# A new order of steps behind the first loads, in a kernel of chunked attention and a phase-mixing layer

## The chip, the cores and the metric

The program runs on one core of a Trainium2 chip. The core has TensorE (matrix products; "PE" in the profile, and "PEld" for its loads of weights), VectorE ("DVE"), ScalarE ("ACT"), GpSimd ("POOL") and SyncE ("SP", which only issues transfers). The engines run side by side, each through its own list of instructions in order, and wait for each other on semaphores. Transfers between the chip's main memory and the core's own memory run on 16 DMA engines. They are issued from POOL (the loads, which also turn 32-bit values into 16-bit ones, and some stores), from SP (stores, and DMA transposes, which turn a tile of 16-bit values around on its way from one place of the core's memory to another) and from ACT (stores). The metric is the time of one execution in microseconds (us); less is better.

## What is computed

Attention inside chunks of 64 positions, for 8 batches, 8 heads, 576 positions and 64 values per head, and then a layer that mixes positions and channels:

```python
scores = scale * np.matmul(q_c, k_c.transpose(0, 1, 2, 4, 3))      # per chunk of 64
scores = scores - np.max(scores, axis=-1, keepdims=True)
attn = np.exp(scores)
attn = attn / (np.sum(attn, axis=-1, keepdims=True) + 1e-09)
out = np.matmul(attn, v_c)                    # then x = out as (batch, position, head*64)
theta = x @ w_theta
zr, zi = x * np.cos(theta), x * np.sin(theta)
y = np.einsum('ts,bsd->btd', w_tok_r, zr) + np.einsum('ts,bsd->btd', w_tok_i, zi)
u = x + y
return u + np.maximum(u @ w_ch, 0.0)
```

## The kernel before

The work goes by pairs of batches, p = 0 to 3. A pair's 2 x 576 positions make nine tiles of 128 rows. They are loaded and attended to in five groups: A (tiles 0 and 1) and B (tiles 2 and 3) of the first batch, C (tiles 4 and 5) and D (tiles 6 and 7) of the second, and M (tile 8), which holds the last 64 positions of both batches.

Everything that the core does is a list of steps, the text `ORDER` (lines 17 to 60). A step such as `V0.0D.4` names a kind of work (V0), a pair and a group (0D) or a pair and a tile, and the places that it uses (4: a bank of TensorE's result memory, of which there are eight, or a slot of the arrays `big`, `mid` or `uT`). The loop at line 711 goes through the list and calls the function of each step; each function gives its instructions to one engine, or to two. So the list is at once the order on every engine. Where a step reads what another wrote, or writes a slot or bank that another still reads, a wait is put in. Nothing else sets the order.

The kinds, in the order in which a group meets them:

- `qk` and `v` (lines 167 and 219) load queries and keys (two transfers of 256 KB; four of 64 KB for M) and values (one of 128 KB and two of 64 KB; two of 64 KB for M), all from POOL; `lw`, `lp`, `lc` load the weights. POOL takes the semaphores of its transfers in turn, eight of them, so that it can be at most eight transfers ahead of the landings.
- `T`, `Tq`, `Tk` (line 291, DVE) turn queries and keys in squares of 32; `S` (line 334, TensorE, 64 products of 32x64 for a group, 32 for M) makes the scores; `E` (line 350, ACT) the exponentials; `V0` and `V1` (line 376, TensorE, 16 products of 64x64 each, 8 for M) the products with the values of four heads; `N0` and `N1` (line 398, DVE) the divisions, which give x.
- `X` (line 415) turns x around on TensorE, and `xv` or `xa` copy the result out on DVE or ACT; or `xd` (line 432) does both in one DMA transpose from SP. `H` (line 453) multiplies by w_theta, `G` (line 474, ACT) takes cosine and sine, `Z` (line 491, DVE) makes zr and zi.
- `TW` (line 253) turns the weights over positions around, `twv` and `twa` copy them out. `Y` (line 540, nine products of 128x512; `Ya`, `Yb`, `Ym` are its parts) mixes the positions for one tile, and needs zr and zi of all its batch's groups and of M; `A` (line 548, DVE) adds x.
- `U` with `uv` or `ua`, or `ud` alone (line 562, a DMA transpose), turns the tile around once more; `W` (line 582, TensorE, four products of 128x512) multiplies by w_ch; `R` (line 586, DVE) makes the result; `st`, `sa` and `sg` (line 664) store it, issued from SP, ACT or POOL.
- `dm` are TensorE products that nobody reads.

A pair's groups are thus at different stages at any moment, and TensorE's list runs through blocks of different kinds and pairs. `crossed` (line 215) says which quarter of the array a chunk's scores go to: for all groups but 0A and 0B the second tile of a group has its two halves exchanged, and its values are loaded in two halves.

Of the kernel before, what the change touches and what calls it, by code (L numbers as in the profile page):

```python
# [17 lines left out]
on.00 init.00 qk1.0A.0 pre.00 qk0.0A.1 qk.0B.2 cy0.0A.3 cv1.0A qk.0M.4 T0.0A.1 S0.0A.0 Tq.0B.0  # L18
v.0A Tk.0B v.0M v.0B Tq.0M.5 lw.03.2 S.0B.2 T1.0A E0.0A.0 V0.0A.0 Tk.0M S1.0A.4 E1.0A S.0M.6
lp.00 E.0M.1 V0.0M.7 N0.0A V1.0M.6 qk.0C.4 N1.0M V1.0A.4 dm.2.0 E.0B.2 lw.01.5 V1.0B.2 V0.0B.0  # L20
N1.0A X.0A.4 qk.1M.1 lw.02.3 N1.0B N0.0B xa.0A.1 X.0B.5 TW.03.3 v.0C N0.0M X.0M.7 xv.0B.2
H1.0A.5 G1.0A.0 H1.0B.0 G1.0B.3 xv.0M.4 Tq.0C.2 Z1.0A H0.0A.7 qk.0D.0 lw.00.6 G0.0A.1 v.0D
twv.03 Z0.0A H.0M.5 H0.0B.4 G.0M.4 TW.01.6 G0.0B.1 Ya.03.3 Tk.0C S.0C.0 Z1.0B twv.01 v.1M E.0C.3
# [3 lines left out]
xv.0C.1 N1.0D V0.0D.4 H.0C.2 G.0C.1 qk.1D.3 V0.1M.6 N0.0D X.0D.4 xv.0D.3 v.1B N0.1M Z.0C Yb.00  # L27
v.1A Ym.00 v.1D H.0D.4 Ya.05.2 T.1B.4 G.0D.5 V1.1M.3 A.00 Ya.06.6 TW.04.0 S.1B.4 Ya.04.7 N1.1M
X.1M.3 E.1B.4 Z.0D Yb.06 T.1A.4 Ym.06 S.1A.4 qk.1C.6 A.06 Yb.05 T.1D.5 xv.1M.3 U.06.6 twv.04
E.1A.1 Ym.05 Ya.07.4 V1.1B.0 qk.2M.3 A.05 ua.06.3 N1.1B V0.1B.5 N0.1B Yb.04 lc.00 S.1D.2 v.1C  # L30
V1.1A.0 Yb.07 qk.2C.5 Ym.07 qk.2D.4 N1.1A E.1D.2 V0.1D.2 N0.1D X.1B.0 xa.1B.4 V1.1D.5 Ym.04
H.1M.1 H.1B.2 qk.2B.0 N1.1D V0.1A.5 A.07 qk.2A.2 qk.3B.1 Y.08.4 T.1C.7 A.04 N0.1A X.1A.5 U.04.6
G.1M.2 Z.1M xv.1A.1 U.00.7 S.1C.0 v.2M G.1B.6 E.1C.4 A.08 X.1D.5 xv.1D.2 v.2B W.06.2 R.06.3
U.07.0 H.1A.4 uv.04.3 V0.1C.2 v.3D uv.07.4 v.2A uv.00.5 W.00.7 G.1A.7 N0.1C U.05.0 U.08.6
uv.08.5 v.2C V1.1C.2 W.01.1 uv.05.6 H.1D.4 N1.1C X.1C.2 Z.1A Z.1B R.01.2 qk.3A.6 W.08.3 xa.1C.4
Y.10.0 H.1C.1 G.1D.7 Z.1D T.2M.8 T.2A.7 W.02.4 S.2M.5 v.3B G.1C.9 Z.1C R.02.4 E.2M.1 Y.13.6 A.13
T.2B.9 S.2A.1 W.04.4 R.00.0 Y.16.5 qk.3D.0 R.04.5 R.08.6 W.05.4 S.2B.6 T.2D.7 E.2B.7 T.2C.2
Y.11.3 A.11 R.05.8 A.16 W.03.6 R.03.9 Y.15.7 A.15 E.2A.10 V1.2A.5 A.10 S.2C.3 E.2C.11 V0.2M.1
N0.2M V1.2M.7 N1.2M Y.14.2 N1.2A V0.2B.3 N0.2B V0.2A.0 V0.2C.6 v.2D Y.17.5 A.14 A.17 V1.2C.2
# [4 lines left out]
W.16.0 st.08 qk.3C.8 T.3M.4 Y.25.1 T.3C.1 Y.24.5 Y.27.4 A.24 ud.13.1 G.2B.5 S.3B.5 A.25 W.14.1  # L44
R.14.3 Y.26.7 Z.2A S.3M.1 E.3B.6 E.3D.1 V1.3D.2 R.16.12 S.3C.5 A.27 Z.2B sa.07 ud.15.2 ud.12.6
ud.10.4 ud.18.5 W.18.0 E.3C.10 E.3M.7 Y.20.4 sa.17 A.26 V0.3M.7 R.18.11 V0.3C.0 N1.3D W.15.5
R.15.5 N0.3C st.14 S.3A.2 E.3A.3 W.12.6 Y.23.5 V1.3M.2 A.20 N0.3M N1.3M W.10.7 st.11 R.10.7
sa.10 R.12.13 V0.3D.3 N0.3D V1.3C.1 ud.25.3 N1.3C Y.28.0 W.13.4 st.16 ud.27.0 V1.3A.2 V0.3B.6
A.28 st.18 R.13.7 N1.3A Y.21.0 A.21 st.02 ud.24.2 Y.22.2 A.22 xd.3M.12 H.3M.0 V1.3B.3 sa.03
W.24.2 N0.3B N1.3B V0.3A.6 N0.3A ud.20.1 G.3M.10 W.25.1 xd.3D.9 H.3D.3 G.3D.7 xd.3C.1 Z.3M  # L50
H.3C.6 G.3C.5 Z.3D A.23 Z.3C ud.21.4 xd.3B.6 W.21.0 ud.22.3 sa.05 H.3B.3 G.3B.7 Z.3B ud.26.2
W.22.6 st.12 Y.34.7 R.25.8 W.26.3 R.24.6 sg.25 R.22.13 Y.35.1 A.35 R.26.1 R.21.8 xd.3A.10 W.27.6
W.20.2 H.3A.3 sg.21 st.01 st.00 Y.36.0 Y.37.1 R.20.0 sa.20 A.34 ud.28.4 W.28.7 ud.23.6 G.3A.7
A.36 Z.3A Y1.31.0 sa.13 Y.38.3 ud.34.3 A.37 ud.35.1 R.28.7 A1.31 st.24 A.38 W.34.0 Y0.31.7 A0.31
sg.22 ud.37.0 W.37.3 W.35.7 R.34.13 R.37.6 st.26 Y.32.0 A.32 U0.31.3 uv0.31.1 R.35.1 U1.31.1
Y.33.4 A.33 st.15 ud.36.4 W.36.7 W.23.3 R.27.5 ud.38.2 sg.35 sa.34 R.23.13 R.36.1 W.38.6 R.38.0
sa.37 sa.28 Y.30.4 Wp.31.6.7 uv1.31 sa.38 A.30 W0.31 ud.32.3 W.32.1 R0.31.7 sa0.31 R.32.6 U.30.6
sa.36 W1.31 uv.30.1 R1.31 st.27 ud.33.6 W.33.4 R.33.0 st.32 sa.33 W.30.6 sg.23 dm.2.7 R.30.13
st1.31 sa.30
# [4 lines left out]
def kernel(  # L64
# [137 lines left out]
    def cast_qk_half(f, engines):  # L202
        def cast(p, g, slot=None):
            if f == 0:
                st["qk", p, g] = big(slot).rearrange(
                    "p (f w h s d) -> p f w h s d", f=2, w=2, h=HH, s=2
                )
            t, to = st.pop(("stage", f)), st["qk", p, g][:, f]
            for w, e in enumerate(engines):
                copy = nc.scalar.copy if e == "a" else nc.vector.tensor_copy  # L210
                copy(out=to[:, w], in_=t[:, w])

        return cast

    def crossed(p, g):

        return int(p > 0 or g not in "AB")

    def load_v(p, g):
# [86 lines left out]
    def qk_t_half(f):  # L306
        def step(p, g, slot=None):
            if f == 0:
# [10 lines left out]
    def score_mms(ps, t, n, heads, cross):  # L319
        for h in range(heads):  # L320
            for e in range(2):
                for c in range(2 * n):
                    r, cc = (c // 2, c % 2) if n == 2 else (0, c)
                    to = cc ^ (r * cross)
                    nc.tensor.matmul(  # L325
                        ps[half[to], r, h],
                        t[quarter[c], 1, h, :, e],
                        t[quarter[c], 0, h, :, e],
                        start=(e == 0),
                        stop=(e == 1),  # L330
                        tile_position=(32 * c, CH * to),
                    )

    def scores(p, g, b):
# [413 lines left out]
```

## Time and profile before

| | |
|---|---|
| three executions | 195.51, 193.31, 194.77 us (median 194.77) |
| the profiled execution, first to last instruction (span) | 191.7 us |
| TensorE's granted clock | 1.000 throughout |
| instructions | 5957, 2579 of them products |
| HBM read and written | 33.06 MB and 9.44 MB |

The page gives the profiled execution's span alone; the executions' own times lie 1.6 to 3.8 us above it, which is what lies around the first and the last instruction and the spread between executions. In the profile's lines "L528" is line 528 of the kernel, "us" after a start is a duration, and what stands in brackets is the time for which the engine stood idle before, with what ended it. A product's record outlasts the time after which the next one may start, so blocks are best timed from start to start, or by the pieces of the chain of waits, which do not overlap.

### The profile page before, as it was taken

The page shows a single profiled execution, that of the slowest core. Times are in us where ns is not written, and L with a number is a line of the kernel's source. Part 1 is how long each engine was busy: PE and PEld are TensorE (multiplying, and loading weights), DVE is VectorE, ACT ScalarE, POOL GpSimd, SP SyncE. Part 2 cuts the span into 40 slices and gives each one's busy share as a digit, 9 for nine tenths or more (in the row PEclk, how much of TensorE's full clock was granted, in tenths as well). Part 3 has the DMA queues.
Part 4 walks back from the last instruction along what each step waited for, and adds up shares of the span by engine and source line. Part 5 has one row for each costly group of instructions (what it writes and reads, how often), then busy time and mean ns, then how long its engine had stood idle before and what let it go on. Part 6 is the DMA issues. An engine that isn't in the chain of part 4 may idle for free.

```text
span 191.7 us, 5957 instructions
## 1 busy us (share of the span) xinstructions
PE 173.9 (91%) x2579; PEld 91.1 (48%) x2579; DVE 138.8 (72%) x255; ACT 81.4 (42%) x100; POOL 88.4 (46%) x125
## 2 busy tenths in 40 slices
PE   0168899999999999999999969999999999999992
PEld 0155455645554655554555425454444444455450
DVE  0564789879779977996885968396686677553782
ACT  3113895476629946803218659142032560400000
POOL 8998289697798955799878000000000001100110
PEclk9999999999999999999999999999999999999999
DMA  5999999999999999999999986497356894885667
GB/s 159 202 157 182 188 132 143 164 177 165 151 153 183 175 182 181 157 116 152 164 133 132 196 145 168 82 197 222 74 158 126 112 281 103 246 230 150 180 173 259
DMA packets 103338, 31.86 MB, mean 166 GB/s; under 512 B 94672, under 2 KB 99152, under 8 KB 103312
## 3 DMA queue, kind: packets, MB, share of 16 engines
q0 software_dynamic: 76048, 17.33, 98.2%
q1 hardware_dynamic: 23872, 9.57, 23.9%
q10 hardware_dynamic: 3392, 4.59, 7.6%
q8 instruction: 20, 0.33, 0.7%
q14 instruction: 6, 0.05, 0.1%
HBM read 33.06 MB, written 9.44 MB: 222 GB/s over the span
## 4 chain that ended last, share of the span: by engine, by line
PE 78%; DMA 8%; DVE 4%; POOL 4%; issue 2%; ACT 1%; DVEq 0%; ACTq 0%; POOLq 0%
PE psum L528 35%; PE psum L573 14%; PE psum L449 12%; PE psum L325 6%; PE psum L389 5%; DMA out_dram<-mid 3%; PE psum L421 3%; DMA mid<-x 2%; DMA v<-in_v_dram 2%; PE psum L264 1%; POOL big L174 1%; PE psum L555 1%; POOL big L179 1%; DVE mid L578 1%; DVE x L406 1%
## 5 line engine op out<-in xcount | busy, mean ns | idle before, releaser
L528 PE MATMUL psum<-zr,wT 128*128 128x512 f16 (+2 forms) x185 | 62.6, 375 | 0.1
L528 PE MATMUL psum<-zi,wT 128*128 128x512 f16 (+2 forms) x184 | 59.6, 374 | 0.0
L528 PEld LDWEIGHTS <-wT 128*128 128x128 f16 (+1 forms) x369 | 31.3, 100 | 32.9 <-issue 0.5
L233 POOL DMA_DIRECT2D v<-in_v_dram x54 | 41.0, 787 | 10.1 <-DMA big<-in_k_dram 4.5
L672 POOL DMA_DIRECT2D out_dram<-mid x5 | 2.7, 551 | 75.3 <-DVE mid L578 75.3
L573 PE MATMUL psum<-wch,uT 128*128 128x512 f16 x140 | 35.1, 380 | 0.0
L550 DVE TENSOR_TENSOR x<-psum,x 128x512 f16<-128x512 f32 x35 | 23.7, 683 | 15.3 <-PE psum L528 15.1
L449 PE MATMUL psum<-wtheta,mid 128*128 128x512 f16 x144 | 33.2, 379 | 1.7 <-DMA mid<-x 1.7
L355 ACT ACTIVATE mid<-psum 128x1024 f16<-128x1024 f32 (+1 forms) x19 | 17.3, 930 | 33.9 <-PE psum L325 32.2
L578 DVE SCALAR_TENSOR_TENSOR mid<-psum,x 128x512 f32<-128x512 f32 (+1 forms) x37 | 23.9, 669 | 7.7 <-PE psum L573 5.6
L406 DVE TENSOR_TENSOR x<-psum,recip 128x512 f16<-128x512 f32 (+1 forms) x40 | 25.5, 638 | 1.4
L286 DVE STREAM_TRANSPOSE big<-big 128x1024 f32<-128x1024 f32 (+3 forms) x25 | 24.7, 1011 | 1.3 <-DMA big<-in_q_dram 0.9
L325 PE MATMUL psum<-big 32*64 32x64 f16 x1152 | 15.3, 199 | 9.5 <-DVE big L286 9.5
L471 ACT ACTIVATE big<-psum,pihalf 128x1024 f16<-128x1024 f32 x14 | 15.6, 1116 | 17.4 <-PE psum L449 17.4
L449 PEld LDWEIGHTS <-mid 128*128 128x128 f16 x144 | 13.9, 98 | 18.1 <-DMA mid<-x 2.2
L325 PEld LDWEIGHTS <-big 32*64 32x64 f16 x1152 | 13.0, 112 | 15.1 <-DVE big L286 10.1
L573 PEld LDWEIGHTS <-uT 128*128 128x128 f16 x140 | 12.4, 98 | 13.4 <-issue 0.8
L152 ACT ACT_TABLE_LOAD x12 | 15.4, 1283 | 6.3 <-DVE recip L404 4.8
L179 POOL DMA_DIRECT2D big<-in_q_dram x15 | 13.8, 920 | 1.7 <-DMA big<-in_k_dram 0.9
L472 ACT ACTIVATE big<-psum 128x1024 f16<-128x1024 f32 x14 | 14.3, 1024 | 0.0
L389 PEld LDWEIGHTS <-mid 64*64 64x64 f16 x576 | 8.9, 113 | 11.4 <-issue 9.0
L389 PE MATMUL psum<-v,mid 64*64 64x65 f16 x576 | 12.2, 202 | 2.0 <-DMA v<-in_v_dram 1.3
(51 smaller groups left out, 135.7 us busy)
## 6 DMA issues: line engine op xcount, KB each, us to landing
big<-in_q_dram POOLq DMA_DIRECT2D x15, 256.0 KB, 6.5
big<-in_k_dram POOLq DMA_DIRECT2D x15, 256.0 KB, 7.0
out_dram<-mid SPq DMA_DIRECT2D x13, 256.0 KB, 2.8
out_dram<-mid ACTq DMA_DIRECT2D x13, 256.0 KB, 3.0
v<-in_v_dram POOLq DMA_DIRECT2D x18, 128.0 KB, 5.7
v<-in_v_dram POOLq DMA_DIRECT2D x36, 64.0 KB, 6.1
out_dram<-mid POOLq DMA_DIRECT2D x5, 256.0 KB, 3.1
out_dram<-mid SPq DMA_DIRECT2D x5, 128.0 KB, 3.0
```

Of the source, the lines that this page charges most:

```text
L179: nc.gpsimd.dma_start(t[:, w].rearrange("p h s d -> p h (s d)"), ap[2 * p + bb, :, s0 : s0 + GT, :].rearrange("h (p s) d -> p h (s d)", s=2),)
L233: nc.gpsimd.dma_start(v16[rows, slot + t, :, 0:D], v[b, :, t0 : t0 + m, :].rearrange("h s d -> s h d"),)
L286: nc.vector.transpose(out.bitcast(FP32).rearrange("p (x l s) -> p x s l", l=32, s=2), in_.bitcast(FP32).rearrange("p (x s d) -> p x s d", ...
L325: nc.tensor.matmul(ps[half[to], r, h], t[quarter[c], 1, h, :, e], t[quarter[c], 0, h, :, e], start=(e == 0), stop=(e == 1), tile_position= ...
L355: nc.scalar.activation(out=eT[:, 0:n].rearrange("p r h i -> p (r h i)"), in_=st.pop(("ps_s", p, g)).rearrange("p r h i -> p (r h i)"), fun ...
L389: nc.tensor.matmul(ps[half[cc], r, h4, :], eT[rows, r, h, :], v16[rows, slot + r, h, 0 : D + 1],)
L406: nc.vector.tensor_tensor(out=x.rearrange("p r (h d) -> p r h d", h=HH), in0=ps[:, :, :, 0:D], in1=recip[:, 0:n].broadcast_to((P, n, HH, D ...
L449: nc.tensor.matmul(ps, xT[:, a, :], wtheta16[:, a, :], start=(a == 0), stop=(a == NDB - 1))
L528: nc.tensor.matmul(ps[half[b]] if j == MID else ps, w, z[:, cols], start=(kt == 0), stop=(kt == 2 * KT),)
L550: nc.vector.tensor_tensor(out=x, in0=st.pop(("ps_y", p, j)), in1=x, op=ALU.add)
L573: nc.tensor.matmul(ps, uT[:, a, :], wch16[:, a, :], start=(a == 0), stop=(a == NDB - 1))
L578: nc.vector.scalar_tensor_tensor(out=out, in0=ps, scalar=0.0, in1=x, op0=ALU.max, op1=ALU.add)
```

## The change

The list `ORDER` is replaced. The same 562 entries of the same kinds stand in it, with few differences: of the copies and stores some go to another engine (from DVE to ACT or back: the copies out after X for 0C, 1A, 1C, 1M, 2A, 2M, after TW for tile block 4 and after U for five tiles; and there are 17 whole stores from ACT instead of 15, 8 from POOL instead of 5, 10 from SP instead of 15). The steps up to `Ya.01`, at the end of the first pair's start, are the same and in the same order, except that `TW.02` now stands ahead of `Ya.01`, and with other slots. Behind that the order is new.

```diff
-on.00 init.00 qk1.0A.0 pre.00 qk0.0A.1 qk.0B.2 cy0.0A.3 cv1.0A qk.0M.4 T0.0A.1 S0.0A.0 Tq.0B.0
+on.00 init.00 qk1.0A.0 pre.00 qk0.0A.1 qk.0B.2 cy0.0A.5 cv1.0A qk.0M.15 T0.0A.3 S0.0A.0 Tq.0B.4 v.0A
...
-Z0.0B Ya.01.6 Yb.01 TW.02.4 twa.02 Z.0M Ym.01 T.1M.2 A.01 Yb.03 V0.0C.0 Ym.03 V1.0C.4 Tq.0D.1
-S.1M.6 E.1M.4 Ya.02.7 Yb.02 Ym.02 N1.0C Tk.0D S.0D.4 N0.0C A.03 TW.00.0 qk.1B.2 A.02 X.0C.3
-lw.04.0 E.0D.3 U.01.6 ua.01.0 U.02.4 ua.02.1 U.03.5 twv.00 Ya.00.0 V1.0D.6 uv.03.2 qk.1A.6
...
+H0.0B.6 G.0M.9 TW.01.2 G0.0B.10 Ya.03.7 Tk.0C S.0C.4 Z1.0B twv.01 v.1M E.0C.11 Z0.0B TW.02.0 Ya.01.6
+Z.0M Yb.03 V0.0C.2 V1.0C.4 twa.02 Yb.01 Ya.02.0 Ym.01 T.1M.16 Yb.02 S.1M.1 Tq.0D.17 E.1M.12 N0.0C
+Tk.0D S.0D.2 E.0D.13 Ym.03 N1.0C TW.00.4 X.0C.1 A.01 A.03 twv.00 Ym.02 A.02 V0.0D.6 N0.0D qk.1B.18
...
-N1.2C N0.2A N0.2C Y.18.4 xd.2C.12 S.2D.2 st.04 qk.3M.2 V1.2B.0 E.2D.1 X.2A.5 W.07.6 N1.2B v.3C
-V0.2D.0 R.07.7 N0.2D V1.2D.2 xa.2A.11 v.3A X.2M.7 X.2B.5 v.3M Y.12.6 A.12 N1.2D H.2A.0 xa.2M.10
-A.18 T.3A.7 H.2M.6 xa.2B.1 G.2M.13 T.3D.5 Z.2M H.2C.4 H.2B.6 G.2A.6 xd.2D.5 ud.16.4 G.2C.0 Z.2C
-ud.17.2 T.3B.9 H.2D.0 W.17.4 S.3D.2 G.2D.4 Z.2D ud.11.6 W.11.5 R.17.5 R.11.13 sa.06 ud.14.3
...
+V1.2B.2 N1.2B N0.2A N1.2C Y.18.0 S.2D.6 V0.2C.1 qk.3A.0 N0.2C X.2A.3 xd.2C.9 A.18 ud.11.9 X.2M.4
+xv.2M.13 E.2D.4 W.07.5 R.07.3 V1.2D.6 V0.2D.1 Y.12.0 T.3D.2 X.2B.4 xa.2B.1 H.2M.5 N1.2D S.3D.6 N0.2D
+H.2C.1 xv.2A.7 qk.3B.3 H.2A.3 ud.17.4 qk.3C.14 G.2M.4 xd.2D.13 W.17.5 G.2C.15 ud.18.2 qk.3M.7 A.12
+H.2D.0 Z.2C Z.2M G.2A.12 W.18.2 T.3C.8 H.2B.3 T.3B.18 ud.15.8 ud.16.1 G.2D.10 Z.2D Y.26.0 A.26 st.06
...
-sa.36 W1.31 uv.30.1 R1.31 st.27 ud.33.6 W.33.4 R.33.0 st.32 sa.33 W.30.6 sg.23 dm.2.7 R.30.13
-st1.31 sa.30
+st.23 W.32.5 R.32.3 sa.22 sa0.31 W.34.6 W.30.3 R.33.12 sa.37 sa.26 sg.32 R.34.13 sg.34 R.30.1 sg.30
+W.36.1 sa.35 R.36.10 sg.36 st.33 dm.2.7 st1.31 sa.27
```

On POOL the values of 3M are loaded much sooner, the pairs' values and queries are exchanged in places, and the last four loads are `qk.3A`, `qk.3B`, `qk.3C`, `qk.3M`. On SP the first transposes stand as `xd.2C`, `ud.11`, `ud.17`, `xd.2D`, `ud.18`, `ud.15`, `ud.16`, and only then comes the first store, `st.06`; before, `st.04` stood between `xd.2C` and `xd.2D`.

The functions change little. Which tile of a group has its halves exchanged now depends on the group (`turned`; the second tile for A and C, the first for B and D), and `load_v` follows it with the same number of transfers:

```diff
-    def crossed(p, g):
-
-        return int(p > 0 or g not in "AB")
+    def turned(p, g, r):
+
+        if p == 0 and g in "AB":
+            return 0
+        return r ^ int(g in "BD")
...
+            parts = []
+            for t in range(2):
+                t0 = s0 + t * P
+                if turned(p, g, t):
+                    parts += [(half[1 - i], t, 2 * p + bb, t0 + i * CH, CH) for i in range(2)]
+                else:
+                    parts.append((slice(0, P), t, 2 * p + bb, t0, P))
...
-        score_mms(ps, t, n, H, crossed(p, g))
...
+    def scores(p, g, b):
+        score_mms([score_parts(p, g, b)], size(g), H)
+
+    def scores_of_two(p, gs, *bs):
+
+        score_mms([score_parts(p, g, b) for g, b in zip(gs, bs)], 2, H)
```

`score_mms` has a loop over groups inside, so that a new kind of step, `SS`, could make the scores of two groups at once; no entry of the new list uses it. In five functions of halves the place is taken from whichever half comes first with a slot (`if slot is not None` for `if f == 0`), and the loop over the list reads names of two groups.

More of the change, by code (lines that the diff above doesn't have):

```diff
@@ L30 @@
[L30 to L35, printed above, removed]
@@ L48 @@
[L48 to L53, printed above, removed]
@@ L322, in score_mms, with score_parts @@
                 for c in range(2 * n):
[L323 to L334, printed above, removed]
+                    for p, g, ps, t in groups:
+                        r, cc = (c // 2, c % 2) if n == 2 else (0, c)
+                        to = cc ^ turned(p, g, r)
+                        nc.tensor.matmul(
+                            ps[half[to], r, h],
+                            t[quarter[c], 1, h, :, e],
+                            t[quarter[c], 0, h, :, e],
+                            start=(e == 0),
+                            stop=(e == 1),
+                            tile_position=(32 * c, CH * to),
+                        )
+    def score_parts(p, g, b):
         n = size(g)
@@ L387, in products @@
                     for cc in range(2):
-                        rows = half[cc ^ (r * crossed(p, g))]
+                        rows = half[cc ^ turned(p, g, r)]
                         nc.tensor.matmul(
@@ L653, in step @@
         def step(p, j, slot=None):
-            if f == 0:
+            if slot is not None:
                 st["o", p, j] = mid(slot, 1, FP32)
```

74 lines of the change are left out of this document (39 added, 35 removed).

## The prediction
> **What bounds the kernel now.** I read the page first (busy shares, the slices, the queues), then the chain of waits in order of time.
>
> ```profile
> span 191.7 us, 5957 instructions
> PE 173.9 (91%) x2579; PEld 91.1 (48%) x2579; DVE 138.8 (72%) x255; ACT 81.4 (42%) x100; POOL 88.4 (46%) x125
> ...
> PE   0168899999999999999999969999999999999992
> ...
> DMA  5999999999999999999999986497356894885667
> ...
> q0 software_dynamic: 76048, 17.33, 98.2%
> ...
> PE 78%; DMA 8%; DVE 4%; POOL 4%; issue 2%; ACT 1%; DVEq 0%; ACTq 0%; POOLq 0%
> ```
>
> TensorE is busy in every slice from the fifth to the last but one, and the chain lies on it for 78%. Beside it the DMA engines are full until slice 23, about 111 us, with POOL's loads (q0). So there are two clocks: TensorE's list, and the landings of the loads, which TensorE must not outrun. A gain can come from less time in TensorE's list, from its stalls, or from the ends. The chain shows all three:
>
> ```profile
> 27.60 0.68 DVE wT L274
> 28.28 0.05 issue
> 28.33 1.90 PE psum L528 x8
> ...
> 36.17 0.73 PE psum L264 x10
> 36.90 0.55 PE psum L421 x8
> ...
> 38.13 0.86 PE psum L528 x4
> ...
> 55.19 0.25 PE psum L389 x16
> ...
> 79.00 2.05 PE psum L528 x9
> 81.04 0.64 PE psum L325 x64
> 81.68 0.97 PE psum L573 x4
> 82.65 1.94 PE psum L528 x9
> 84.59 0.86 PE psum L573 x4
> ...
> 94.26 0.51 PE psum L389 x48
> ...
> 107.49 4.72 DMA mid<-x
> ...
> 112.26 1.90 PE psum L449 x8
> ```
>
> The reader is to see three things. A W block (L573) takes 0.86 after another large block, and 0.97 after an S block (L325); a Y block (L528) takes 1.94 or 2.05 in the same way; three V blocks in a row (L389 x48) take 0.51, where one by itself takes 0.25. So each boundary between S, V and the large blocks costs about 0.10. Without it S is 0.54, V 0.15, TW (L264) 0.62, X (L421) 0.45, a Y block's four products 0.87 and its last 0.22. And there is one long wait in mid-run, H.2D (L449) for the DMA transpose xd.2D.
>
> **The change, part by part.**
>
> *Boundaries.* The work on TensorE is the same. I count the places in the two lists where TensorE goes from one of the three kinds (S; V; all others) to another: 83 before, 59 after, because V blocks stand in threes and S blocks in twos and threes. 24 x 0.10 = -2.4 us, all of it on the path, since TensorE is the path. Ends: -0.6, if S next to S or V costs what it costs beside a large block, and -2.6.
>
> The Trainium skill, TensorEngine Tiling (Array Packing), section Key Properties, says that changing the tiling mode drains TensorE; its page TensorE: Matmul & The Clock Gate, section Single matmul latency, gives a constant of 398 cycles at 2.4 GHz, 0.17 us, for what a product takes beyond its columns. Taken as the price of a boundary that would be an estimated 24 x 0.17 = 4.1 us, and a sum 1.7 lower. The trace has 0.10 there, and it decides.
>
> *Stalls that go.* What released H.2D is seen in SP's own waits and in TensorE's row:
>
> ```profile
> SPq L433 <- DMA out_dram<-mid: 5.1, 1, 5.1
> ...
> 112.26 1.90 PE L449 MATMUL psum<-wtheta,mid 128*128 128x512 f16 x8 [1.67 <-DMA mid<-x]
> ```
>
> xd.2D writes mid slot 5, from which st.04 had to be stored first. In the new list no store is on SP before xd.2D, and xd.2D goes to slot 13. That frees TensorE's 1.67 and, since the next block's start is usually hidden, 1.8 from start to start. The wait for a weight copy at 28.28 (0.2) goes too, as TW.02 now stands in it. Together -2.0.
>
> *Stalls that come, 1: group 0D.* Up to S.0C both lists are alike on every engine, and POOL's list is alike up to qk.1A, so these loads land as they do now:
>
> ```profile
> 27.52 0.71 PE L325 MATMUL psum<-big 32*64 32x64 f16 x64
> ...
> 34.49 0.71 DVE L286 STREAM_TRANSPOSE big<-big 128x512 f32<-128x512 f32 x1 [0.26 <-DMA big<-in_k_dram]
> ...
> L233 POOL DMA_DIRECT2D v<-in_v_dram x2: 764/764/765, 31.3 to 32.0; - x2
> ...
> DMA to landing us min/median/max: 6.4/6.6/6.8
> ```
>
> Tk.0D waits for its keys until 34.49 and ends at 35.2; the last values of 0D, issued at 32.0, land 6.8 later, at 38.8. Old TensorE had Y, U and V of other groups to do until then. From S.0C (27.52) to V0.0D the new list has three S (1.6), two TW (1.2), five blocks of four Y products (4.35), three Ym (0.7), two V (0.3), one X (0.45) and eight boundaries (0.8): 9.4 us, so V0.0D is reached at 36.9 and cannot start before 38.9. +2.0 (0.7 of it shows at S.0D, which waits for Tk.0D). U and Ya.00, which covered this, now stand behind V0.0D. Bounds: 1.5, if TensorE is itself late by the smaller waits that it has today, and 2.2. This lateness then covers the later loads: v.3M now lands before v.1A, which would otherwise hold up V1.1A.
>
> *Stalls that come, 2: xd.2C.* It is issued when N0.2C is done, and H.2C waits for it. Between V0.2C and H.2C the new list has 6.3 us of TensorE's work (three V, three X, W, Y, H.2M, S.3D, five boundaries). How soon a division follows its V, and how long a transpose takes:
>
> ```profile
> 100.08 0.21 DVE L404 RECIPROCAL recip<-psum 128x8 f32<-128x8 f32 x1
> 100.32 0.69 DVE L406 TENSOR_TENSOR x<-psum,recip 128x512 f16<-128x512 f32 x1
> ...
> mid<-x SPq DMA_TRANSPOSE x1, 6.1
> ...
> mid<-x SPq DMA_TRANSPOSE x1, 4.7
> ...
> mid<-x SPq DMA_TRANSPOSE x7, 3.9
> ```
>
> V1.2B starts 0.4 before its reciprocal, so a division is done 1.3 after its V starts, and 4.9 are left for the transpose. Issued at 100.1 among the loads it took 6.1; issued at 107.5, at the loads' end, 4.7; the median of all is 3.9. In the new list xd.2C is issued at about 101.4 with 3B, 3C and 3M still to load, so I take 6.1: +1.2, with ends 0 and 1.5. What follows on SP (ud.11, ud.17, xd.2D) is issued 1.25 apart, and TensorE comes to it 6 us or more after its issue.
>
> *Smaller waits.* Z.2D, Z.3C and Z.3D now come late for their Y, because the H blocks of four groups stand close together and ACT (two passes of about 1.1) and DVE (two of 0.7) work them off in turn; and E.1C comes behind a table load. I put them at +0.4 from the engines' running sums, with ends 0 and 1.2. All other copies that go from one engine to another have slack of 0.2 us or more by the same sums, and I cost them at nothing; their cover is TensorE's own backlog. The new slots, the other halves turned, and the functions' loops issue the same instructions: 0.
>
> *The tail.* Now it is W.30, R.30, a store from ACT; then it is W.36, R.36, a store from POOL.
>
> ```profile
> 181.19 0.69 DVE L578 SCALAR_TENSOR_TENSOR mid<-psum,x 128x512 f32<-128x512 f32 x1 [0.44 <-PE psum L573]
> ...
> 182.18 0.54 POOL L672 DMA_DIRECT2D out_dram<-mid  x1 [2.31 <-DVE mid L578]
> ...
> L672 ACTq DMA_DIRECT2D out_dram<-mid x2: 338/338/339, 188.0 to 188.6; - x2
> ...
> DMA to landing us min/median/max: 2.1/2.1/2.1
> ...
> out_dram<-mid POOLq DMA_DIRECT2D x5, 256.0 KB, 3.1
> ...
> 188.00:190.00 2.00, 0.14 (x1) 0.00 (x0) 0.59 (x1) 0.00 (x0) 0.00 (x0) 1.00 1.00 369
> ```
>
> POOL begins 0.3 after the result is written, and its stores land after 3.1, ACT's last after 2.1: +1.3. Besides, sa.26, sa.35 and sa.27 wait behind sa.37 on ACT's queue, so four stores start at once near the end. At 369 GB/s a store of 256 KB takes the engines 0.71, and results come every 0.86, so some of the backlog is still there: I take +1.5 in all, with ends 0.3 and 2.5.
>
> The Trainium skill, DMA: Bandwidth & Descriptors, section Specifications, puts the first byte of a POOL transfer only 0.4 us behind one of SP or ACT; by that the tail would cost an estimated 0.4, and the sum would be 191.3. The rows say more, and I keep them.
>
> Sum: 191.7 - 2.4 - 2.0 + 2.0 + 1.2 + 0.4 + 1.5 = 192.4, 0.7 above the span of before. The span lies 3.1 below the median, 194.77; with the same 3.1 around it, 195.5.
>
> **The rivals.**
>
> *Faster: the two transfers are cheaper than their rows.* If xd.2C lands in 4.7 and the last store as ACT's would (0.3 left of the 1.5), the span is 192.4 - 1.2 - 1.2 = 190.0, time 193.1; without the smaller waits 192.7. For it: 4.7 was measured with loads still running. Against it: all of the POOL stores' median.
>
> *Slower: TensorE outruns the loads again, at group 2B.* v.2B now comes behind v.2C, v.2D, qk.2C, qk.2D and v.3A. Against the loads that were in before the last of v.2C,
>
> ```profile
> L233 POOL DMA_DIRECT2D v<-in_v_dram x2: 731/735/739, 83.0 to 83.7; - x2
> ...
> DMA to landing us min/median/max: 4.0/4.2/4.4
> ```
>
> at 83.7 + 4.0 = 87.7, it is qk.3B and v.3D (768 KB) less and v.2D, v.3A and v.3M (640 KB) more, so v.2B lands near 87.6; TensorE's running sum reaches V0.2B at 88.7. If the loads fall 1.1 behind, the margin is gone, and each further us is a stall. One load of values comes about every 2 us, so the price is up to 2: span 194.4, time 197.5. Against it: a margin of 1.1 where nothing ahead of it on POOL waits for a slot.
>
> *The change does not do what it says:* if S and V next to their own kind pay the boundary too, 2.4 come back: span 194.8, time 197.9. Against it: the row of three V in 0.51.
>
> **How the numbers follow.** Forecast 0.51, faster rival 0.24, slower rival 0.18, no gain from boundaries 0.07. About 1% is what a measurement of this kernel can tell from no change. Faster by over 1% (below 192.8) is half of the faster rival and the forecast with its stalls at the lower ends: 0.21. Slower by over 1% (above 196.7) is most of the other two rivals, and a forecast with its ends added up: 0.24. The rest, 0.55, is within 1%. The range goes from the faster rival without the smaller waits and 0.5 below, 192.2, to the slower rivals, 197.7. The forecast's own range is 193.7 to 197.0.
>
> **What would show it.** In the profile after: V blocks in threes at 0.5; TensorE idle at about 35 and 37.5 for a key transpose and for v; idle before L449 at about 106 for a DMA transpose; no wait of SP's transposes for a store near 107; the last store issued by POOL some 2 us behind the last L573 block and landing about 3 later. The prediction is wrong if the loads of 0D land sooner than 38.8, if xd.2C lands within 4.9, or if a new stall of over 1 us stands anywhere else.

## The result, and the profile after

The changed kernel takes 203.72 us (median of 4 runs, 201.17 to 204.60); the kernel before took 194.98 beside it (193.31 to 195.51). The ratio is 1.038, with a 95% interval of 1.029 to 1.047: slower by 3.8%. It goes by the executions of 201.17 and 203.04 alone, since the other two are of a slower state. The forecast was 195.5, with a range up to 197.7. The profiled execution of the changed kernel is the longest of the four, 204.60 us; its span is 202.8, 11.1 above the 191.7 of before. So the 11.1 that is taken apart below is more than the 7.4 between the means behind the ratio (202.1 and 194.7). In the changed kernel the line numbers are 1 to 8 higher: scores L326, products with v L397, transposes of x L429, theta L457, mixing L536, channel weights L581, DMA transposes L441 and L571, stores L680.

From the page of the changed kernel: span, the slices of TensorE, of its clock and of the DMA engines, the queue of instructions, the shares of the chain, and the landing times of two groups of transfers.

```profile
span 202.8 us, 5929 instructions
...
PE   0168999899999999979995799999999999999910
...
PEclk9999999999999999999999699999999999999995
DMA  6999999999999999999999965208987610897893
GB/s 167 194 150 170 183 141 166 147 178 170 134 137 166 175 146 86 168 146 143 167 183 157 138 165 161 78 3 190 156 201 171 157 66 0 249 210 178 223 345 119
...
q8 instruction: 20, 0.33, 0.7%
...
PE 49%; DMA 23%; POOL 13%; DVE 5%; issue 3%; ACT 2%; POOLq 0%; SPq 0%
...
out_dram<-mid POOLq DMA_DIRECT2D x6, 256.0 KB, 6.7
```

Against the page of before: TensorE's share of the chain went from 78% to 49%, and that of the DMA engines from 8% to 23%. Slice 23 (112 to 117 us) has a clock of 0.6; before, every slice had full clock. In slice 34 (167 to 172) nothing at all is moved, and in the last but one, where TensorE is all but through, 345 GB/s are.

The chain of waits of the changed kernel, in order of time (start, duration, what it is):

```profile
99.56 0.51 PE psum L397 x46
...
104.12 8.66 DMA mid<-x
112.78 0.04 issue
112.83 5.31 PE psum L457 x16
...
136.79 0.51 PE psum L397 x48
```

Three V blocks in a row take 0.51, as forecast. But xd.2C takes 8.66 us where 6.1 was forecast, and the sixteen products behind it take 5.31, or 0.33 each in place of 0.215.

TensorE's own rows there (start, duration, line, what released it in brackets):

```profile
91.32 0.70 PE L397 MATMUL psum<-v,mid 64*64 64x65 f16 x46 [0.92 <-DMA v<-in_v_dram]
...
108.26 0.61 PE L429 MATMUL psum<-id,x 128*128 128x128 f16 x8 [1.16 <-DVE recip L412]
...
112.83 1.14 PE L457 MATMUL psum<-wtheta,mid 128*128 128x512 f16 x3 [2.46 <-DMA mid<-x]
```

These are three new waits. V0.2B waits for its values, V.2B; this is the slower rival of the prediction. H.2C waits for xd.2C. And X.2B stands 1.16 idle for something that the row names wrongly: the reciprocal that it names was over by 107.7, and nothing that X.2B reads or writes was late.

All in all, from start to start of blocks and by the block prices of the prediction (us):

| where | forecast | measured |
|---|---|---|
| boundaries on TensorE, 83 to 59 | -2.4 | -2.5 |
| old waits that go | -2.0 | -2.6 (1.8 of it H.2D) |
| group 0D | +2.0 | +1.7 |
| H.2C waits for xd.2C | +1.2 | +2.5 |
| lower clock behind that wait | - | +1.7 |
| V0.1C (0.8) and V0.2B (1.6) wait for values | (rival, for V0.2B) | +2.5 |
| X.2B | - | +1.3 |
| smaller waits; a later start of the full clock | +0.4 | +1.0 |
| tail, last W block to the end: 5.0 to 10.7 | +1.5 | +5.7 |
| sum | +0.7 | +11.3 (span +11.1) |

Two of these rows hang together. By the prediction TensorE has work for 4.9 of the time that xd.2C takes, so a transfer of 8.66 would cost 3.8; the stop at X.2B (1.3) and the wait at H.2C (2.5) make up just that. So the 1.3 lies inside the time in which xd.2C is awaited, and would not come back by itself; experiment 3 shows it.

### The profile page after: what moved, and what is told of

The parts are those of the page before. It is cut to its first block, busy times and chain, and to the rows that moved or that the text cites. A ratio compares the mean times of both kernels' runs of the same rounds, so it can differ in the third digit from the quotient of the medians.

```text
span 202.8 us, 5929 instructions
## 1 busy us (share of the span) xinstructions
PE 174.7 (86%) x2579; PEld 93.1 (46%) x2579; DVE 137.1 (68%) x253; ACT 82.3 (41%) x102; POOL 91.3 (45%) x130
## 4 chain that ended last, share of the span: by engine, by line
PE 49%; DMA 23%; POOL 13%; DVE 5%; issue 3%; ACT 2%; POOLq 0%; SPq 0%
PE psum L536 26%; DMA big<-in_k_dram 12%; PE psum L581 9%; PE psum L457 7%; DMA v<-in_v_dram 7%; POOL v L233 5%; DMA mid<-x 4%; POOL big L177 3%; PE psum L326 3%; PE psum L397 3%; POOL big L243 1%; POOL big L172 1%; ACT big L479 1%; DVE x L414 1%; DVE zr L506 1%
## 5 line engine op out<-in xcount | busy, mean ns | idle before, releaser
L536 PE MATMUL psum<-zr,wT 128*128 128x512 f16 (+2 forms) x185 | 62.2, 375 | 0.0
L536 PE MATMUL psum<-zi,wT 128*128 128x512 f16 (+2 forms) x184 | 59.4, 374 | 0.1
L536 PEld LDWEIGHTS <-wT 128*128 128x128 f16 (+1 forms) x369 | 31.6, 100 | 32.9 <-issue 0.4
L457 PE MATMUL psum<-wtheta,mid 128*128 128x512 f16 x144 | 34.9, 393 | 2.5 <-DMA mid<-x 2.5
L680 POOL DMA_DIRECT2D out_dram<-mid x6 | 3.3, 560 | 73.3 <-DVE mid L586 73.2
L581 PE MATMUL psum<-wch,uT 128*128 128x512 f16 x140 | 33.9, 379 | 0.0
L326 PE MATMUL psum<-big 32*64 32x64 f16 x1152 | 14.6, 199 | 10.5 <-DVE big L286 10.5
L457 PEld LDWEIGHTS <-mid 128*128 128x128 f16 x144 | 14.1, 101 | 19.0 <-DMA mid<-x 2.6
L581 PEld LDWEIGHTS <-uT 128*128 128x128 f16 x140 | 13.2, 98 | 14.9 <-issue 0.4
L326 PEld LDWEIGHTS <-big 32*64 32x64 f16 x1152 | 12.7, 112 | 14.9 <-DVE big L286 10.8
L506 DVE TENSOR_TENSOR zr<-x,big 128x1024 f16<-128x1024 f16 x14 | 9.5, 681 | 9.0 <-ACT big L479 8.9
L397 PE MATMUL psum<-v,mid 64*64 64x65 f16 x576 | 11.7, 201 | 4.1 <-DMA v<-in_v_dram 3.2
```

The source lines that it names most:

```text
L326: nc.tensor.matmul(ps[half[to], r, h], t[quarter[c], 1, h, :, e], t[quarter[c], 0, h, :, e], start=(e == 0), stop=(e == 1), tile_position= ...
L397: nc.tensor.matmul(ps[half[cc], r, h4, :], eT[rows, r, h, :], v16[rows, slot + r, h, 0 : D + 1],)
L457: nc.tensor.matmul(ps, xT[:, a, :], wtheta16[:, a, :], start=(a == 0), stop=(a == NDB - 1))
L536: nc.tensor.matmul(ps[half[b]] if j == MID else ps, w, z[:, cols], start=(kt == 0), stop=(kt == 2 * KT),)
L581: nc.tensor.matmul(ps, uT[:, a, :], wch16[:, a, :], start=(a == 0), stop=(a == NDB - 1))
```

## The experiments

All are made from the changed kernel by moving entries of its list, unless another origin is given. "Tail" is the time from the start of the last W block to the end of the span. A ratio is against the kernel before, run beside it; the changed kernel's is 1.038.

**1. The tail: whose stores?** Three kernels. In the first the last stores change their queue (sa.35, sa.27, st.33 and st1.31 also stand a little earlier in the list, in the same order on their queues):

```
-sg.28 ... sg.38 ... sg.32 ... sg.34 ... sg.30 ... sg.36
+sa.28 ... st.38 ... sa.32 ... st.34 ... sa.30 ... st.36
```

> Only the last stores are issued differently: the six of POOL's queue (of 28, 38, 32, 34, 30, 36) by SP and ACT, each behind its result as in the changed kernel. What is watched is the tail, from the start of the last W block to the end of the span: 10.7 us in the changed kernel, 5.0 before. Theory A, POOL's queue is slow to deliver (its stores landed 6.7 after issue, in the median): the tail falls to about 6.5, the time by 3 to 4 us. Theory B, seven W blocks in a row give a result every 0.86 us and three old results (26, 35, 27) are held back, so the DMA engines are behind whoever issues: the tail stays between 9.5 and 11, the time within 1 us, and the stores of SP and ACT land 5 to 7 us after issue. The stretch before the tail is untouched: H.2C again waits over 2 us for xd.2C, V0.2B over 1 us for v.2B.

Measured: 203.23 us, ratio 1.045 (1.033 to 1.057); the tail is 9.3, a little under theory B's 9.5. Four other kernels whose tail is that of the changed kernel have 10.0 to 10.6, so POOL's queue is worth about 1 us, and the stores of SP and ACT land up to 5.7 after issue. Theory A falls as the main cause. Ahead of the tail this profile, of 201.6 us, has the waits of the changed kernel's: 1.28 at X.2B, 2.85 at H.2C, and half clock from 112.7 on. In the second kernel three held-back stores go out early:

```
+R.25.13 sa.26 st.14 sa.21 sa.08 ... R.27.2 sa.27 ... R.35.9 sa.35
-sa.37 sa.26 ... sa.35 R.36.10 ... st1.31 sa.27
+sa.37 ... R.36.10 ... st1.31
```

> sa.26, sa.27 and sa.35 go out right behind their results (at about 173, 179 and 186 us) and not at 190; POOL's stores stay. Tail in the changed kernel 10.7 us. Theory B (the DMA engines are behind with the stores): 768 KB less to move at the end, at about 0.75 us for 256 KB, so the tail falls by 2 to 2.5, to about 8.4. Theory A (POOL's queue): the last store, from POOL, still lands about 7 us after its issue, and the tail stays above 10.

Measured: 208.12 us, ratio 1.070 (1.061 to 1.078). The tail fell to 7.2, more than theory B said, but TensorE stood still for 6 us before it. From TensorE's and VectorE's timeline:

```profile
183.56 0.69 DVE L586 SCALAR_TENSOR_TENSOR mid<-psum,x 128x512 f32<-128x512 f32 x1 [6.38 <-DMA out_dram<-mid]
...
184.90 1.44 PE L581 MATMUL psum<-wch,uT 128*128 128x512 f16 x3 [5.98 <-DVE x L558]
```

R.27 writes the slot from which sa.08 is stored. With sa.26 ahead of it on ACT's queue, sa.08 was issued at 175.5 (172.7 before) and landed at 183.5 (176.3), for it came among transposes and other stores. VectorE waits for it, and A.30 and W.35 behind VectorE. So the store that was moved was not what cost; the one behind it was.

The third kernel moves seven stores, with that in mind:

```
+ud.21.5 st.14 ... sa.02 sa.08 sa.11 ... sa.21 sa.26 ... R.27.2 sa.27 ... R.22.8 sa.22 ... R.35.9 sa.35
```

> Seven stores of old results are moved to where their queue and the DMA engines are free: st.14, sa.08 and sa.11 into the stretch from 162 to 172 us, in which the changed kernel moves nothing at all (0 GB/s), sa.26, sa.27, sa.22 and sa.35 behind their results, each behind the stores whose slots are wanted first. Theory B: the tail is a backlog of stores, made by this order; three stores (768 KB) fewer after 189 us, at 0.7 to 0.8 us each, bring the tail from 10.7 (9.2 without POOL's queue) to 8 to 8.5, and no new wait comes on TensorE between 172 and 190 us, unlike with the three stores put ahead of sa.08, where R.27 waited for sa.08's slot and TensorE stood for 6 us. Rival: the stores that remain are slow whatever stands before them (each lands 5 to 7 us after its issue), and the tail stays above 9.5.

Measured: 200.22 us, ratio 1.031 (1.024 to 1.037); the tail is 7.7 (8 to 8.5 was expected), and no new wait comes behind 172 us. The interval of the ratio still meets the changed kernel's, so the 3 us are shown by the profile and not by the times. The last column of these windows is GB/s, the one before it the DMA engines' share; the first window is the gap, the second the tail. The changed kernel:

```profile
162.00:172.00 10.00, 9.91 (x50) 4.72 (x49) 5.73 (x10) 0.93 (x2) 0.00 (x0) 1.00 0.12 44
...
190.00:200.00 10.00, 3.55 (x17) 1.41 (x15) 3.57 (x6) 0.00 (x0) 3.26 (x6) 0.93 0.91 296
```

With the stores spread:

```profile
162.00:172.00 10.00, 9.91 (x47) 4.41 (x45) 5.90 (x10) 1.86 (x2) 0.00 (x0) 1.00 0.36 120
...
190.00:200.00 10.00, 4.48 (x21) 1.86 (x19) 3.87 (x6) 0.00 (x0) 4.01 (x8) 0.97 0.71 228
```

In the kernel before it was 214 in the first window. In the changed list no store is issued from 161.3 to 172.3: st.14 stands on SP behind ud.37, which waits until 172.8 for A.37 (behind R.21 on VectorE), and sa.08 and sa.11 stand on ACT behind sa.21, which waits for R.21. What did not go then goes at the end, beside seven W blocks that give a result every 0.86. Theory B holds.

**2. The transpose of 2C.** TensorE turns x of 2C itself:

```
-X.2A.3 xd.2C.9 A.18 ... Y.12.0 T.3D.2 X.2B.4 xa.2B.1 H.2M.5 N1.2D S.3D.6
+X.2A.3 A.18 ... Y.12.0 X.2C.5 xa.2C.9 T.3D.2 X.2B.4 xa.2B.1 N1.2D S.3D.6 H.2M.5
```

> x of group 2C is turned by four plus four TensorE transposes and copied by ACT, in place of the DMA transpose xd.2C, which landed 8.7 us after its issue; S.3D goes ahead of H.2M, to leave the copy its time. Theory: that one transfer costs 2.5 us of wait at H.2C and, by the lower clock behind that wait (eight products of H.2C in 3.07 us in place of 1.73, and H.2A), another 1.7; the new block costs 0.45. So the time falls by 3 to 4 us, the granted clock stays near 1 between 108 and 120 us, and H.2C takes 1.7. Rival: TensorE then runs into what is late behind it (xd.2D, the loads of 3B and 3C, the tail with its stores), and the time falls by less than 1.5 us; or the clock falls there without the wait, and 1.7 stay.

Measured: 203.48 us (199.89 to 205.19, 4 runs; no ratio on record). The median is 0.2 and the lowest 1.3 below the changed kernel's, so the rival's side by the time. H.2C no longer waits, but X.2C, which now comes first, does:

```profile
109.57 1.87 PE L429 MATMUL psum<-id,x 128*128 128x128 f16 x16 [2.64 <-DVE x L558]
```

The row names A.18, over by 104.5; the clock falls behind this wait too. From the start of Y.12 to that of W.17 it is 12.0 us, against 13.0 in the changed kernel: 1.0 is gained in place. This wait stands at the same instruction, counted from the program's start, as that of X.2B. That led to the next theory.

**3. The wait that the row names wrongly.** TensorE's instructions are read by DMA: the page has 20 reads of 16 KB (q8), and 20 times 16 KB is 64 bytes for each of its 5,158 weight loads and products, so 256 to a read. Between 105 and 108 us, in the DMA view of the changed kernel, one of them stands among the loads:

```profile
q0 software_dynamic: 2106, 0.53, 180.4%
q8 instruction: 1, 0.02, 2.0%
```

Counted in blocks of 256, so that X.2B begins one, the trace's DMA records give this (us; first the entry of the block before, then the read, then TensorE's first product of the new block):

```
kernel                 entered   read            goes on at      behind the read
changed kernel         102.16    106.02-106.97   X.2B  108.26    1.29
POOL's stores moved    101.88    105.64-106.57   X.2B  108.10    1.53
x of 2C by TensorE     101.99    106.66-108.07   X.2C  109.57    1.50
loads mixed             98.92    102.84-103.82   X.2B  105.05    1.23
```

The read begins 3.8 to 4.7 after the entry and lasts 0.9 to 1.4, and TensorE goes on 1.2 to 1.5 later. So with a read as late as this a block that TensorE is through with in less than about 6 us stops it; this one, with S.2D and three V blocks, takes 4.6. A short block alone does not: the one ahead of it in the changed kernel (from 96.99 to 102.16) is read 1.9 after its entry, and one of 3.5 us in the kernel before (from 99.16 to 102.65) 0.7 after, and neither brings a stop. What made this read late is not shown. The test moves the block's edge, and nothing else:

```
-pre.00 qk0.0A.1
+pre.00 dp.36.6 qk0.0A.1
```

The new entry makes 36 products on zeros, of 64 columns each.

> The changed kernel with 36 small products more (64 columns of zeros, nothing read from them) ahead of the first scores, where TensorE is idle anyway; nothing else differs, but every later instruction of TensorE stands 72 places further on in its stream. Theory F: TensorE's instructions come in blocks of 256, read by DMA (20 reads of 16 KB on queue 8); in the changed kernel and in all four experiments so far TensorE stood 1.4 to 2.8 us ahead of the same instruction, the first of the block after Y.12, until 1.2 to 1.5 us after the end of such a read, which itself began 3.8 to 4.7 us after the block before was entered. By F the stop moves with the block's edge: it lies inside V1.2D, five products in, 1 to 1.7 us long and 1.2 to 1.5 behind the end of a read, and X.2B starts right behind Y.12. Rival G: X.2B waits for an operand or a bank; then the 1.4 us stand ahead of X.2B as before.

TensorE's timeline in that kernel:

```profile
102.60 0.25 PE L397 MATMUL psum<-v,mid 64*64 64x65 f16 x6
103.06 0.41 PE L397 MATMUL psum<-v,mid 64*64 64x65 f16 x26 [0.22 <-issue]
...
105.14 0.38 PE L536 MATMUL psum<-zr,wT 128*128 128x512 f16 x1
105.36 0.61 PE L429 MATMUL psum<-id,x 128*128 128x128 f16 x8
...
112.17 1.46 PE L457 MATMUL psum<-wtheta,mid 128*128 128x512 f16 x3 [4.70 <-DMA mid<-x]
```

X.2B follows Y.12 without a gap, and the stop is in V1.2D, six products in, 1.46 behind a read that ended at 101.60. It is smaller than expected, 0.4, since that read began 2.8 after the entry. Rival G falls. The time, 203.18 (one run), did not move: H.2C waits for xd.2C all the same, now for 4.8. xd.2C took 10.0 here, 5.1 more than the 4.9 that TensorE has work for, and 0.4 and 4.8 are 5.2: with or without the stop at X.2B, H.2C starts when the transfer lands.

The edge seven blocks earlier says the same. In the changed kernel and in this one:

```profile
55.42 0.22 PE L397 MATMUL psum<-v,mid 64*64 64x65 f16 x2 [0.17 <-issue]
```

```profile
53.51 0.39 PE L536 MATMUL psum<-zr,wT 128*128 128x512 f16 x1 [0.48 <-issue]
```

The small stop in V0.1B, 1.46 behind a read that ended at 53.96, is one block later in the list here, ahead of Yb.04, 1.45 behind a read that ended at 52.06.

**4. The loads.** The same eleven places in the list, q and k in turn with v:

```
-qk.2B v.2M qk.2A v.2A v.2C v.2D qk.2C qk.2D v.3A v.2B v.3B
+qk.2B v.2M qk.2A v.2B qk.2D v.2A qk.2C v.2C v.2D v.3A v.3B
```

> POOL's eleven loads from qk.2B to v.3B are issued in another order, q and k in turn with v, in the same places of the list: qk.2B v.2M qk.2A v.2B qk.2D v.2A qk.2C v.2C v.2D v.3A v.3B. Theory C: the loads fall behind because four loads of values in a row (three pieces of 64 to 128 KB each) leave too little under way on POOL's queue; the trace has 70 GB/s between 76 and 80 us for them, against 137 to 160 around. Then no four-us stretch between 68 and 92 us is below 110 GB/s, the last load lands at 111 to 112 us, not 113.6, V0.2B's wait of 1.6 goes, and the time falls by 1.6 to 3. Rival D: values are slow to move however they are mixed; the last load lands at 113 or later, V0.2B's wait goes by the order alone, another group's block (2C or 2D, whose values now come later) takes part of it, and the time falls by 0 to 1.6.

Windows of the changed kernel (as above; POOL's busy time and count stand ahead of the clock):

```profile
72.00:76.00 4.00, 4.00 (x20) 1.86 (x19) 3.92 (x9) 3.14 (x4) 1.51 (x3) 1.00 2.13 137
76.00:80.00 4.00, 4.00 (x81) 1.99 (x79) 4.00 (x6) 3.61 (x4) 3.62 (x5) 1.00 1.04 70
```

and with the loads mixed:

```profile
76.00:80.00 4.00, 4.00 (x81) 1.99 (x79) 4.00 (x6) 3.97 (x5) 2.94 (x5) 1.00 2.01 172
...
84.00:88.00 4.00, 4.00 (x110) 2.28 (x109) 3.44 (x5) 1.51 (x2) 3.96 (x6) 1.00 2.08 100
```

The last load lands at 109.8, not 113.6, V0.2B does not wait, and the last W block starts 2.8 sooner. Theory C holds for 76 to 80; the low stretch moved to 84 to 88, where four loads of values now stand in a row (I had said none below 110). Behind it lies POOL's issuing: in the changed kernel v.2D's first two pieces are issued 0.3 after the landing of the transfer eight issues earlier (71.94 and 72.23, 74.66 and 74.94). That POOL has at most eight under way was not tried by itself. The time, 201.57 us, has the ratio 1.038 (1.030 to 1.047): the 2.8 of this profile cannot be told in the times, which spread by 2 to 3 us.

**5. The clock.** Eleven products on zeros are put in the wait for xd.2C:

```
-N0.2D H.2C.1
+N0.2D dm.11.1 H.2C.1
```

> The changed kernel with eleven products on zeros (512 columns, 0.215 us each, 2.4 in all) on TensorE between S.3D and H.2C, in the bank that H.2C writes next: TensorE works through the time in which it waits for xd.2C. Theory: the clock falls to half for 3.4 us because TensorE stood still for 2.5 us shortly before; then the wait stays (H.2C starts at about 112.8, when xd.2C lands) but the granted clock stays at 1 through 112 to 120 us, H.2C takes 1.73 and not 3.07, and 1.3 to 1.7 us go. Rival: the clock falls there for another reason (the stop ahead of X.2B alone, or a reading of some other unit), and H.2C keeps its 3 us.

Two windows, the clock in the third column from the right; first the changed kernel, then this one:

```profile
112.00:116.00 4.00, 3.17 (x9) 1.23 (x10) 0.00 (x0) 0.49 (x2) 0.00 (x0) 0.65 1.34 123
```

```profile
112.00:116.00 4.00, 4.00 (x20) 1.78 (x19) 0.69 (x1) 1.87 (x2) 0.00 (x0) 1.00 1.43 127
```

H.2C still starts at 112.2, when xd.2C lands, but takes 1.74 and not 3.07, and the last W block starts 2.1 sooner (1.7 against H.0M's start, which came 0.4 sooner). So the standing still lowered the clock. The ratio is 1.043 (1.037 to 1.049): here too the times do not show it.

**6. The kernel before, without its one long wait.** In two ways:

```
-xd.2C.12 S.2D.2 st.04 ... V1.2D.2 ... A.12 N1.2D
+A.14 st.04 ... xd.2C.12 S.2D.2 ... V1.2D.2 N1.2D ... A.12
```

> The kernel before, with two steps moved: st.04 (its result is ready at 84) is issued before xd.2C, right behind A.14, and N1.2D stands right behind V1.2D, so that xd.2D is issued at about 103 and not at 107.5. Theory: the wait of H.2D for xd.2D behind st.04 was worth 1.8 us, as the prediction has it, and going by itself it makes the kernel before faster by 1.5 to 1.9 us (ratio 0.990 to 0.992). Rival: xd.2C or the loads become later by as much (H.2C has 0.8 us in hand), or xd.2D takes 8 us among the last loads, as xd.2C did in the changed kernel; then the time stays within 0.5 us.

Measured: 195.54 us, ratio 1.007 (1.003 to 1.011). Its chain of waits:

```profile
104.08 7.54 DMA mid<-x
111.62 0.05 issue
111.66 1.90 PE psum L447 x8
```

xd.2D was issued 3.4 sooner than before and landed 0.6 sooner, 0.9 behind the last load. The wait for st.04 was only the first of two; the loads were the next. That profile has a span of 190.8, 0.9 below before's; the ratio, 0.7% the other way, I cannot explain. The executions spread from 192.53 to 197.49 (before's beside them from 192.05 to 196.36).

```
-H.2M.6 ... G.2A.6 xd.2D.5 ud.16.4
+H.2M.6 X.2D.2 xv.2D.5 ... G.2A.6 ud.16.4
```

> The kernel before, with x of group 2D turned by TensorE (eight transposes, 0.45 us, behind H.2M) and copied by VectorE, in place of the DMA transpose xd.2D for which H.2D waits 1.8 us. Moving st.04 out of its way left 1.0 of that wait, since the transpose then took 7.5 us among the last loads. Theory: with no transfer in it the whole wait goes, less the 0.45 of the new block: 1.3 us, ratio 0.992 to 0.995, which is more than the changed kernel got from the same place. Rival: the four transposes behind xd.2D, now issued 5 us sooner among the loads, delay xd.2C or the loads, and it stays within 0.4 us.

The wait is gone; H.2C, H.2B and H.2D run without a break:

```profile
109.00 5.34 PE L447 MATMUL psum<-wtheta,mid 128*128 128x512 f16 x24
```

From H.2A to W.17 it is 8.4 us, against 9.6 before, so 1.2 is gained there; but the ratio is 1.000 (0.997 to 1.003). In the profiled execution H.0M starts 1.6 later than in before's (25.68, not 24.10), which uses up the gain; where the 1.2 goes in the other runs isn't settled.

**7. Together.**

> Three edits together: loads in the mixed order, x of 2C turned by TensorE, stores spread. If they stand beside each other: the mixed loads took 2.8 off the start of the last W block, the turned 2C 1 to 2, the stores 2 to 2.5 off the tail, so 5.5 to 7 us less than the changed kernel, 195 to 197, about the time of before. If each only moves the wait on (TensorE earlier at the next late transfer or instruction block), it is 198 to 200. The stop of 1.4 us or more behind Y.12 for the block of instructions stays in either case, with the lower clock behind it.

Measured: 197.58 us, ratio 1.021 (1.015 to 1.027), a little above the first of the two cases: tail 7.5, V0.2B's wait gone, the stop now ahead of X.2C, 2.2, and the clock low behind it.

> The three edits together, and the last stores on SP's and ACT's queues in place of POOL's, each behind its result. Theory: with the backlog smaller POOL's part of the tail shows by itself: its stores land 3.1 us after issue with little beside them, SP's and ACT's 2.1; the tail falls from 7.5 to between 6 and 6.7, the time by about 1 us against the three edits. Rival: what is left of the tail is stores queued behind each other alone, and it stays at 7 to 7.7.

Measured: 196.38 us, ratio 1.007 (1.004 to 1.011), tail 6.7, as the theory has it. The stop ahead of X.2C was 1.8 in this run, and the clock stayed up. The last kernel takes 64 instructions out of the dense block:

```
-R.07.3 V1.2D.6 V0.2D.1 Y.12.0 ... xa.2B.1 N1.2D S.3D.6 H.2M.5 N0.2D H.2C.1
+R.07.3 Y.12.0 ... xa.2B.1 V1.2D.6 N1.2D V0.2D.1 N0.2D H.2M.5 S.3D.6 H.2C.1
```

> The four edits together, and V1.2D and V0.2D (64 of TensorE's instructions in 0.3 us) stand behind X.2B and no longer ahead of Y.12. Theory F: the edge of the block of 256 then lies right behind V1.2D, and the three us of Y.12, X.2C and X.2B run ahead of it; the read itself comes when it came, so TensorE, which stood 1.8 us ahead of X.2C with the four edits, stands 0.6 to 1.2 us behind V1.2D, and H.2C starts 0.7 to 1 us sooner. The time falls by 0.5 to 1 us, to between 195 and 196, still not below the kernel before. Rival: another wait (the division of 2D ahead of S.3D and H.2C, the copies) takes all of it; H.2C starts no sooner against H.0M's start, and the time stays.

```profile
106.56 0.32 PE L397 MATMUL psum<-v,mid 64*64 64x65 f16 x16
108.49 0.32 PE L397 MATMUL psum<-v,mid 64*64 64x65 f16 x16 [1.61 <-issue]
```

The stop is where theory F puts it, right behind V1.2D and 1.46 behind the end of the read (107.03). But it is 1.8 long, not 0.6 to 1.2: the read began 4.4 after the block's entry and took 1.5. From V0.2C's start to H.2C's it is 8.7 us, as with the four edits (8.6), so nothing is gained in place. Against H.0M's start H.2C comes 0.5 sooner, but that was there before V0.2C. Measured: 195.42 us, ratio 1.005 (1.001 to 1.008). So by the ratios (1.038, then 1.005) the four edits and this one give back seven eighths of what the change lost. No kernel of this study is faster than the one before.

## Why the prediction was wrong

- *Boundaries (-2.4).* Right: -2.5, at 0.10 each, from the rows of V blocks in threes. The estimate of 4.1 from the Trainium skill, TensorE: Matmul & The Clock Gate, section Single matmul latency, is not borne out.
- *Stalls that go (-2.0).* Right in the changed kernel, where st.04 no longer stands before xd.2D. But experiment 6 shows that this wait had a second one behind it: of 1.8 only 0.8 went with st.04 alone.
- *Group 0D (+2.0, ends 1.5 and 2.2).* Right: 1.13 at S.0D and 0.53 at V0.0D, as v.0D landed at 38.91 (38.9 was forecast).
- *xd.2C (+1.2, ends 0 and 1.5).* The mechanism was right, its size wrong: 3.8 in all (2.5 at H.2C and the 1.3 at X.2B that lies in the same wait), and 1.7 more by the clock. The step that failed is "so I take 6.1": the upper end came from the longest transpose seen, issued at 100.1, while this one was issued 4 us later. In the six kernels made from the changed one that keep it, it took 8.8 to 10.0 us. Nearer to it would have been the distance to the end of the loads, which the same page shows, and a wait of over 2 us on TensorE has a price of its own behind it.
- *The slower rival, group 2B (chance 0.18).* It came true, and V0.1C's wait of 0.8 for values was named by nothing: v.2B landed at 91.3, not 87.6. The estimate counted bytes and left out that loads of values in a row bring only 70 to 137 GB/s; "nothing ahead of it on POOL waits for a slot" overlooked that POOL can wait for its own earlier transfers.
- *The tail (+1.5, ends 0.3 and 2.5).* The largest error: 5.7. The mechanism, a backlog of stores, was named, but only three held-back stores were counted. The step that failed is that the stores' issue times were not followed through the three queues from 155 on: each queue stands behind one waiting entry until 172, and 0 GB/s in a window is the sign. The +1.3 for POOL's queue set the median of POOL's stores, 3.1, against the last one of ACT, 2.1; on the same page ACT's median is 3.0:

```profile
out_dram<-mid ACTq DMA_DIRECT2D x13, 256.0 KB, 3.0
```

- *"All other copies ... I cost them at nothing."* The reads of TensorE's instructions were not costed, though the page had their queue: 1.3 at X.2B, hidden here in the wait for xd.2C, but 2.2 to 2.6 with the clock fallen behind it where x of 2C was turned by TensorE (experiment 2 and the three edits).

No wait that the forecast named was of the wrong kind. But the four large costs (xd.2C, v.2B, the instruction block, the stores) are all waits on the same DMA engines, and three of them I had priced by rows in which the others were absent; the fourth I had not priced.

## What to carry to other kernels

Where the DMA engines are full, price a transfer on the critical path by the time at which the queue ahead of it ends, not by the duration of a like transfer at another time, and give it no end of the range that assumes otherwise. Follow every store to its issue through the in-order queue that it stands in: one entry that waits holds those behind it, and with them the buffers that later results need. A denser order saves TensorE's switches, but it can also use up an instruction block before the next has been read; count instructions as well as microseconds between two waits.

## What the runs showed of the hardware

- TensorE's instructions come in blocks of 256, 16 KB each. Where it stopped at an edge behind 100 us, the read had begun 2.8 to 4.7 us after the block before was entered and taken 0.9 to 1.5, and TensorE went on 1.2 to 1.5 later; a read that began 0.7 to 1.9 after brought no stop. Where an edge was moved, the stop moved with it (twice, by 36 products and by 64 instructions).
- TensorE's granted clock fell to half for 3.41 us after it had stood still for 2.0 to 4.7 us in one piece (the changed kernel and seven of the experiments; for 6.83 us after the 6.0 of experiment 1's second kernel); after 1.5 to 1.7 us it did not (the one with zeros and the last two). The Trainium skill, TensorE: Matmul & The Clock Gate, section HAM oscillation — how this bites in real kernels, warns of gaps above about 3.4 us; here a shorter one was enough.
- The record of the clock shows why. Each stretch at full clock between two changes is a whole number of 3.41 us (92.16 is 27 of them). Counted in such windows from the first full speed on, in all 14 traces, the clock fell at the end of every window in which TensorE's products stood still for 2.02 us or more, and of none in which they did for 1.95 or less. So it is the idle time within one window that counted. The nearest two of mid-run, three edits and four (busy time and count of TensorE, ..., then the clock, third from the right):

```profile
103.80:107.22 3.42, 1.40 (x8) 0.53 (x7) 3.35 (x7) 0.00 (x0) 0.00 (x0) 1.00 1.78 178
107.22:110.63 3.41, 3.41 (x82) 2.80 (x82) 0.43 (x1) 2.35 (x3) 0.00 (x0) 0.50 0.45 48
```

```profile
105.47:108.88 3.41, 1.76 (x20) 1.15 (x18) 3.17 (x7) 0.33 (x1) 0.00 (x0) 1.00 1.54 154
108.88:112.30 3.42, 3.41 (x79) 1.95 (x78) 0.00 (x0) 3.39 (x5) 0.00 (x0) 1.00 0.21 36
```

- At the start the clock's record first has full speed between 18.5 and 24.4 us, by the run; H.0M then starts between 24.1 and 26.1. That is up to 2 us between profiled executions whose lists do nearly the same up to there. Each kernel has one profile, so that one kernel's executions differ by as much is not shown; if they do, it hides gains of 1 to 2 us in the times. The same page, section Part 1: The HAM clock gate (the "warmup" mystery), has a free-running window of 3.41 us, which fits.
- A DMA transpose took 8.7 to 10.0 us among the last loads, 3.2 when issued behind them (xd.2D at 113.6, where TensorE turned 2C).
- Stores of 256 KB on POOL's queue landed 6.7 us after issue (median) in the crowded tail, and 3.1 before. Moving them to SP and ACT took the tail from between 10.0 and 10.7 to 9.3, and from 7.5 to 6.7: about 1 us, less than the 1.3 of the prediction and more than the 0.4 between the first bytes in the Trainium skill, DMA: Bandwidth & Descriptors, section Specifications.
